# A transformer layer on one core: eight PSUM banks in one stock, and a first chunk transposed in two halves

## The chip, the core and the metric

The kernel runs on one core of a Trainium2 chip. The metric is the device time of one execution in microseconds (us). The engines are TensorE (PE; its weight loads are a row of their own, PEld), VectorE (DVE), ScalarE (ACT), GpSimd (POOL) and SyncE (SP), which issues most DMAs. PSUM, where matmuls write, has eight banks, each of 512 fp32 numbers on each of 128 partitions.

## The reference

```python
# x (1, 2048, 448); 16 heads of 28; F = 1792; every input is bf16
mod = silu(c) @ w_mod                      # six vectors of 448: sa, ca, ga, sb, cb, gb
h = layernorm(x) * (1 + ca) + sa
q, k, v = split(h @ wqkv)
# token s attends to s, s-2, s-4, ... s-14 (8 keys, those below 0 masked)
x = x + ga * (attention(q, k, v) @ wo)
h = layernorm(x) * (1 + cb) + sb
out = x + gb * (silu(h @ w1) @ w2)
```

## The kernel before

The 2048 tokens go through in four chunks of 512. Even and odd tokens are kept apart ("parity"), since the keys of a token have its own parity; a chunk is four tiles of 128 tokens, two of each parity. D = 448 is held as three k-tiles of 128 rows and a rest of 64, in an order of rows in which the two parities (or the two halves of F) use opposite halves of the rest tile, so that 64-row matmuls can run in pairs on the two halves of the array.

For each chunk: **norm1** (statistics per token, by DVE's `bn_stats` where `HOW1` has "b", by ACT's accumulating Identity and Square where it has "a"; a power on POOL for the reciprocal root; then the normalized tile xn), a transpose of xn (on PE for chunk 0, by DMA for the others), a modulation with (1 + ca) and sa that gives h; **project** (four groups ps_qk for q and k, cast to SBUF; two or three blocks ps_v). Attention goes in nine blocks b of up to 128 queries, for each parity: logits ps_l (16 small matmuls into two double tiles), Exp on ACT into p, a multiplication by a 0/1 mask on DVE, P.V on PE into ps_o with a column of ones for the sum, reciprocal and normalization on DVE into o, a DMA transpose into oT. Then **out_proj** (ps_wo, two tiles per 256 tokens, added to x by DVE), norm2, **ffn1** (seven groups ps_h of two 512-wide halves, Silu on ACT into hid) and **ffn2** (four tiles ps_y of 14 matmuls each, added to x by DVE into ot, stored by SP). The gates ga and gb are multiplied into wo and w2 beforehand, from two matmul groups ps_g.

A group with 64-row parts is made by `phases`: eight matmuls ("straight"), a drain that counts a semaphore, then six ("crossed") that wait for it. Other work can be queued between the two.

Everything is recorded as operations of a `Plan`, with their inputs and the buffers that they take and give back. What runs on each engine, and in which order, is written out in `ORDER`: a list of operation numbers, where a letter picks DVE (v) or ACT (a) for an operation that may run on either. Semaphores between engines are put in by the Tile framework from what each instruction reads and writes.

PSUM before: the pool `big` has three buffers of two banks (all groups of `phases`, the logits, the transposes of chunk 0, the warm-up matmuls), the pool `one` two buffers of one bank (P.V, ps_y, gates, modulation columns). The buffers turn round in the order in which they are asked for:

```python
    def bigt(name):
        return big.tile([128, 2, 512], F32, name=name, tag="big")

    def onet(name):
        return one.tile([128, 512], F32, name=name, tag="one")
```

Lines of the profile that matter here: L399 warm-up matmuls, L427 modulation columns, L443 gates, L524 transposes and L531/L533 their modulation, L561/L563 the padding of wqk into wp, L625 ps_qk, L645 ps_v, L673 ps_l, L681 Exp, L705 mask, L731 ps_o, L736/L737 reciprocal and normalization, L761 ps_wo, L764 its addition, L789 ps_h, L797 Silu, L809 ps_y, L814 its addition. ps_t is the tile of the transposes. When all is done a check of the sums picks, in case of extreme values, a slower path, which does not run here.

Of the kernel before, what the change touches and what calls it, by code (L numbers as in the profile page):

```python
# [7 lines left out]
BF16 = mybir.dt.bfloat16  # L8
F32 = mybir.dt.float32
# [27 lines left out]
WARM, JUNK = 7, 10  # L37
HOW1 = ("bbbb", "bbbb", "bbaa", "bbaa")
# [64 lines left out]
class Plan:  # L103
# [94 lines left out]

    def emit(self, order):
        self.rank()  # L200
        if order:
            seq = []
            for w in order.split():
                o = self.ops[int(w.rstrip("vap"))]
                o["eng"] = {"v": "dve", "a": "act", "p": "pool"}.get(w[-1], o["on"][0][0])
                seq.append(o)
            assert len(seq) == len(self.ops) == len({o["i"] for o in seq})
        else:
            _, got = self.order({o["i"]: o["rank"] for o in self.ops})
            seq = [self.ops[i] for i in got]  # L210
            for o in seq:
                o["at"], o["eng"], o["end"] = got[o["i"]]
        for o in seq:
            for r in o["take"]:
                o["slot"][r] = self.free[r].pop(0)
            o["fn"](o)
            for other, r in o["give"]:
                self.free[r].append(other["slot"][r])


def layer(ctx, tc, io, safe):
# [9 lines left out]
    big = ctx.enter_context(tc.tile_pool(name="big", bufs=3, space=PSUM))  # L231
    one = ctx.enter_context(tc.tile_pool(name="one", bufs=2, space=PSUM))
# [8 lines left out]
    def bigt(name):  # L241
        return big.tile([128, 2, 512], F32, name=name, tag="big")

    def onet(name):
        return one.tile([128, 512], F32, name=name, tag="one")
# [87 lines left out]
    P.resource("dma", 8)  # L333
    begin = P.op(("sp", 1630.0), none)
# [60 lines left out]
    def warm_up(n):  # L395
        if not warm:
            warm.append(bigt("ps_w"))
        for _ in range(n):
            T.matmul(warm[0][:, 0, :], lhsT=junk[:, 0:128], rhs=junk, start=True, stop=True)  # L399
    w_first = P.op(("pe", 600.0), none, take=("big",))  # L400
# [9 lines left out]
    def c_cols(o):  # L410
        box["c"] = one.tile([128, 512], F32, name="ps_c", tag="one")
        T.matmul(box["c"][:, 0:KT], lhsT=sc4[:], rhs=ident[0:KT, 0:KT], start=True, stop=True)
# [4 lines left out]
    def mod_cols(vecs, dst0, loads):  # L417
# [3 lines left out]
        def mm(o):  # L421
            ps[0] = one.tile([128, 2, KT], F32, name="ps_m", tag="one")
# [14 lines left out]
    def gate(i, v, loads):  # L437
        ps = {}

        def mm(o):  # L440
            ps[0] = onet("ps_g")
# [9 lines left out]
    class Norm:  # L451


        def __init__(self, us, src, after=(), n=2, how="bbbb", scratch=None):
# [14 lines left out]
            def mean(o, j):  # L469
# [11 lines left out]
            def shift(o, j, b):  # L481
# [13 lines left out]
            for j in range(0, 4, n):  # L495
                at, b = range(j, j + n), how[j] == "b"
                if b:
                    st = [P.op(("dve", 728.0), lambda o, j=i: stat(o, j), [src[us[i]]]) for i in at]
                    m = st
                else:  # L500
                    st = [P.op(("act", 600.0), lambda o, j=i: total(o, j), [src[us[i]]]) if how[j] == "a" else src[us[i]] for i in at]
                    m = [P.op(("dve", 62.0), lambda o, j=j: mean(o, j), st)]
                    st = [P.op(("act", 665.0), lambda o, j=i: square(o, j), m) for i in at]
                g = P.op(("dve", 62.0), lambda o, j=j: guard(o, j), st)
                r = P.op(("pool", 720.0), lambda o, j=j: rstd(o, j), [g])
                s = P.op(("dve", 62.0), lambda o, j=j, b=b: shift(o, j, b), [r])
                for i in at:
                    self.nr.append(P.op(either(704.0, 322.0), lambda o, j=i, b=b: norm(o, j, b), [r, s] + self.nr[:1], take=() if i else ("xn",)))

        def on_pe(self, order, out_of, view, waits, two=False):  # L510

            box, trs = self.box, []


            parts = ((0, 1), (2, 3)) if two else ((0, 1, 2, 3),)

            def tr(o, j):
                if j == 0:
                    for i in range(len(parts)):
                        box[i] = big.tile([128, KT // len(parts), 512], BF16, name="ps_t", tag="big")  # L520
                at = slice(128 * order[j], 128 * order[j] + 128)
                for i, ks in enumerate(parts):
                    for k in ks:
                        T.transpose(box[i][:, k - ks[0], at], box["x"][:, j, 128 * k:128 * k + 128], ident[:])  # L524

            def mod(o, i, ks):
                for k in ks:
                    out_, in_ = out_of(k), view(box[i][:, k - ks[0], :])
# [5 lines left out]
            for j in range(4):  # L534
                trs.append(P.op(("pe", 240.0), lambda o, j=j: tr(o, j), [self.nr[j]] + (trs[-1:] or self.after), take=() if j else ("big",) * len(parts),
                                give=((self.nr[0], "xn"),) if j == 3 else ()))
            self.done = []
# [407 lines left out]
```

## Time and profile before

| | us |
|---|---|
| median of three runs | 174.2 (173.69 to 174.68) |
| the profiled execution | 174.89 |
| its span | 173.2 |
| busy PE / ACT / DVE / POOL | 163.9 / 113.7 / 104.5 / 15.6 |
| first ps_v, first ps_qk, first ps_h start | 11.74, 14.40, 67.02 |
| last matmul ends | 168.7 |

The granted clock of PE is 0.999. Of the costliest groups, ps_y has 224 matmuls, ps_h 392, ps_qk 224, ps_wo 112, ps_v 126 and ps_o 288. The page gives busy time as a share of the span; matmuls are pipelined, so a matmul's own duration (0.35 us and more) is longer than the distance from one to the next, which is what counts in a dense stretch. In the slices, a digit is the busy share of a 4.33 us slice in tenths. In the timeline a row has start, duration, engine, line, operation, tiles, count, and in brackets the idle time before it with what ended it.

### The profile page before, as it was taken

The numbers are of one execution on the slowest core, as the hardware profiler recorded it, in microseconds if no ns is written. First come the engines' busy times: TensorE is split into PE (matmuls) and PEld (weight loads), VectorE is DVE, ScalarE is ACT, GpSimd is POOL, SyncE is SP. The second block draws the span as 40 slices with busy tenths as digits, with TensorE's granted clock in tenths as the row PEclk, the third lists the DMA queues.
The fourth block names the chain that finished last, engine by engine and source line by source line (L and its number), as shares of the span: only waits on it lengthen the run. The fifth ranks groups of instructions, "written<-read, shape, count | busy, mean of one in ns | idle before, by whom it ended". The sixth has DMA issues, their size and how long they took to land.

```text
span 173.2 us, 4260 instructions
## 1 busy us (share of the span) xinstructions
PE 163.9 (95%) x1770; PEld 81.0 (47%) x1771; DVE 104.5 (60%) x258; ACT 113.7 (66%) x157; POOL 15.6 (9%) x38
## 2 busy tenths in 40 slices
PE   7999999889999989999999999999999999999990
PEld 2544443345644544454554445555444444444540
DVE  5898988999999889328477325898361231100221
ACT  2269999977895845999998669644429933356000
POOL 3432311000001020002000000012001100000000
PEclk9999999999999999999999999999999999999999
DMA  5993999499935542001500303225200060200111
GB/s 181 341 308 89 225 234 257 149 240 141 318 81 127 143 97 53 4 0 25 126 2 4 81 0 83 54 57 113 61 28 28 1 149 30 80 0 2 32 57 36
DMA packets 33347, 17.47 MB, mean 101 GB/s; under 512 B 24297, under 2 KB 32937, under 8 KB 33321
## 3 DMA queue, kind: packets, MB, share of 16 engines
q1 hardware_dynamic: 33168, 16.90, 37.2%
q8 instruction: 16, 0.26, 0.7%
q10 hardware_dynamic: 152, 0.23, 0.5%
q14 instruction: 11, 0.08, 0.2%
HBM read 9.12 MB, written 1.84 MB: 63 GB/s over the span
## 4 chain that ended last, share of the span: by engine, by line
PE 70%; DVE 16%; DMA 7%; ACT 2%; POOL 2%; issue 2%; ACTq 0%
PE ps_y L809 25%; PE ps_h L789 25%; PE ps_wo L761 7%; DMA x_all<-in_A_x_dram 5%; PE ps_qk L625 4%; PE ps_v L645 3%; DVE st L463 3%; DVE p L705 2%; PE ps_o L731 2%; PE ps_l L673 2%; DMA oT<-o 2%; POOL rs L479 2%; DVE qk L629 2%; DVE o L737 1%; DVE x_all L764 1%
## 5 line engine op out<-in xcount | busy, mean ns | idle before, releaser
L809 PE MATMUL ps_y<-w,both 128*128 128x448 bf16 x224 | 44.7, 353 | 0.0
L789 PE MATMUL ps_h<-h,w 64*128 64x512 bf16 x392 | 44.3, 376 | 0.0
L797 ACT ACTIVATE both<-ps_h 128x1024 bf16<-128x1024 f32 x28 | 27.5, 1019 | 14.9 <-PE ps_h L789 14.6
L681 ACT ACTIVATE p<-ps_l 128x896 bf16<-128x896 f32 (+1 forms) x36 | 31.4, 927 | 5.8 <-PE ps_l L673 5.6
L809 PEld LDWEIGHTS <-both 128*128 128x128 bf16 x224 | 20.8, 98 | 20.2 <-issue 1.5
L789 PEld LDWEIGHTS <-w 64*128 64x128 bf16 x392 | 19.6, 94 | 21.8 <-issue 0.6
L814 DVE TENSOR_TENSOR ot<-ps_y,x_all 128x448 bf16<-128x448 f32 x16 | 10.0, 623 | 29.7 <-PE ps_y L809 29.6
L479 POOL TENSOR_TENSOR rs<-rs,negh 128x2 f32<-128x2 f32 x16 | 12.7, 793 | 120.0 <-DVE rs L476 82.4
L625 PE MATMUL ps_qk<-h,wp 64*128 64x512 bf16 x168 | 19.6, 377 | 0.5 <-ACT qk L629 0.4
L705 DVE TENSOR_TENSOR p<-p,maskb 128x1792 bf16<-128x1792 bf16 (+1 forms) x18 | 19.5, 1098 | 0.8 <-ACT p L681 0.8
L625 PEld LDWEIGHTS <-wp 64*128 64x128 bf16 x224 | 10.8, 94 | 13.4 <-issue 1.8
L473 ACT ACTIVATE screp<-x_all,mv 128x448 bf16<-128x448 bf16 x16 | 10.7, 666 | 4.3 <-DVE mv L470 4.1
L761 PE MATMUL ps_wo<-wo,oT 64*128 64x448 bf16 x112 | 12.7, 350 | 0.4 <-DMA oT<-o 0.4
L629 ACT CAST qk<-ps_qk 128x1024 bf16<-128x1024 f32 x10 | 9.9, 1007 | 3.7 <-PE ps_qk L625 3.7
L764 DVE SCALAR_TENSOR_TENSOR x_all<-ps_wo,x_all 128x448 bf16<-128x448 f32 x16 | 9.3, 620 | 4.5 <-PE ps_wo L761 4.5
L737 DVE TENSOR_TENSOR o<-ps_o,rc 112x448 bf16<-112x448 f32 (+1 forms) x18 | 11.2, 624 | 0.6
L645 PE MATMUL ps_v<-wv,h 64*128 64x448 bf16 x98 | 11.2, 350 | 0.4 <-ACT p L681 0.3
L731 PEld LDWEIGHTS <-p 128*128 128x128 bf16 x288 | 8.6, 96 | 5.3 <-DVE p L705 2.5
L731 PE MATMUL ps_o<-v,p 128*128 128x29 bf16 x288 | 10.0, 176 | 1.0 <-DVE p L705 0.9
L489 ACT ACTIVATE xn<-x_all,nm,rs 128x512 bf16<-128x512 bf16 x10 | 8.0, 807 | 3.6 <-DVE nm L482 3.2
L736 DVE RECIPROCAL rc<-ps_o 112x16 f32<-112x16 f32 (+1 forms) x18 | 4.5, 250 | 8.9 <-PE ps_o L731 8.9
L399 PE MATMUL ps_w<-both 128*128 128x512 bf16 x26 | 8.4, 479 | 1.3 <-DVE both L293 1.3
(85 smaller groups left out, 141.2 us busy)
## 6 DMA issues: line engine op xcount, KB each, us to landing
out_dram<-ot SPq DMA_DIRECT2D x16, 112.0 KB, 1.8
both<-in_w_mod_dram SPq DMA_DIRECT2D x2, 672.0 KB, 4.9
x_all<-in_A_x_dram SPq DMA_DIRECT2D x3, 448.0 KB, 5.7
w<-in_B_w_dram SPq DMA_DIRECT2D x3, 448.0 KB, 5.2
w<-in_B_w_dram SPq DMA_DIRECT2D x1, 896.0 KB, 7.1
both<-in_w_mod_dram SPq DMA_DIRECT2D x2, 336.0 KB, 5.5
w<-in_B_w_dram SPq DMA_DIRECT2D x1, 672.0 KB, 5.1
wv<-in_A_wqkv_dram SPq DMA_DIRECT2D x2, 224.0 KB, 5.6
```

The lines of the kernel that those rows point to most:

```text
L479: G.tensor_tensor(out=rs[:, j:j + n], in0=rs[:, j:j + n], in1=negh[:, 0:n], op=ALU.pow)
L625: return T.matmul(ps[:, j, :], lhsT=w.rearrange("p h d -> p (h d)"), rhs=h[rows, :, t, 128:128 + CP], start=start, stop=stop)
L629: copy_on(o)(out=qk[:, :, g, :, s0:s0 + CP], in_=ps[:].rearrange("p j (t s) -> p j t s", t=2))
L645: T.matmul(ps[:, par, 0:D], lhsT=h[rows, par, t, b0:b0 + 128], rhs=wv[rows, t, :], start=start, stop=stop)
L681: S.activation(out=out_, in_=ps[:, :, 0:4 * nq].rearrange("p j (g q) -> p j g q", q=nq), func=ACTF.Exp, scale=SCALE)
L705: V.tensor_tensor(out=p, in0=p, in1=maskb[:, 1 if b == 0 else 0, 0:nq].unsqueeze(1).to_broadcast([128, H, nq]), op=ALU.mult)
L731: T.matmul(ps[:, h, 0:DH + 1], lhsT=p[:, at:at + 128], rhs=v[:, h, 0:DH + 1], start=True, stop=True)
L737: V.tensor_tensor(out=box["o"][0:nq, off:off + D].rearrange("p (h d) -> p h d", d=DH), in0=ps[0:nq, :, 0:DH], in1=r.unsqueeze(2).to_broadc ...
L761: T.matmul(ps[:, par, 0:D], lhsT=oT[rows, t, par, s0:s0 + 128], rhs=wo[rows, par, t, :], start=start, stop=stop)
L789: return T.matmul(ps[:, j, :], lhsT=w, rhs=h[rows, :, t, :], start=start, stop=stop)
L797: silus[k].append(P.op(("act", 904.0), lambda o, i=i, box=box: S.activation(out=hid[:, k % 2, :, i, :], in_=box["ps"][:], func=ACTF.Silu), ...
L809: T.matmul(box["ps"][:, 0:D], lhsT=hid[:, k % 2, f % 2, f // 2, 128 * j:128 * j + 128], rhs=w2[:, f // 2 + 7 * (f % 2), :], start=(f == 0) ...
```

## The change

PSUM becomes four tiles of two banks, made once. A double tile is one of them, a single tile is half of one. Which of them an operation takes is written into `ORDER` behind a slash (0 to 3 for doubles, 0 to 7 for singles), so that the eight banks are one stock:

```diff
-    big = ctx.enter_context(tc.tile_pool(name="big", bufs=3, space=PSUM))
-    one = ctx.enter_context(tc.tile_pool(name="one", bufs=2, space=PSUM))
+    banks = ctx.enter_context(tc.tile_pool(name="banks", bufs=1, space=PSUM))
...
+    pairs = [banks.tile([128, 2, 512], F32, name=f"ps{i}") for i in range(4)]
+
+    def bigt():
+        return pairs[P.bank("big")]
+
+    def onet():
+        q = P.bank("one")
+        return pairs[q // 2][:, q % 2, :]
```

The output projection takes two singles instead of a double, and gives each back after its own addition. Chunk 0 is transposed and modulated in two halves of two tiles each, each in one bank, with eight modulations of 256 columns instead of four of 512; the V of block 0 needs the first half alone. The statistics of the fourth token tile move from DVE to ACT, and the warm-up shrinks:

```diff
-WARM, JUNK = 7, 10
-HOW1 = ("bbbb", "bbbb", "bbaa", "bbaa")
+WARM, JUNK = 7, 4
+HOW1 = ("bbba", "bbbb", "bbaa", "bbaa")
...
+        def on_pe(self, out_of, waits):
+            self.done = []
+            for i in range(2):
+                box, trs = {}, []
+                def tr(o, j, i=i, box=box):
+                    if j == 0:
+                        box["t"] = onet().bitcast(BF16).rearrange("p (k n) -> p k n", k=KT)
+                    for k in range(KT):
+                        T.transpose(box["t"][:, k, 128 * j:128 * j + 128], self.box["x"][:, 2 * i + j, 128 * k:128 * k + 128], ident[:])
...
-        box, first, m = phases(wo_mm, "ps_wo", D, need + wo_gated)
+        box, first, m = phases(wo_mm, D, need + wo_gated, True)
         for par in range(2):
-            x1_done[u + par] = P.op(("dve", 543.0), lambda o, par=par: add(o, par), [m])
-        P.op(("none", 0.0), none, [x1_done[u], x1_done[u + 1]], give=((first, "big"),))
+            x1_done[u + par] = P.op(("dve", 543.0), lambda o, par=par: add(o, par), [m] + ([x1_done[u]] if par else []), give=((first, "one"),))
...
-            box, first, m = phases(vmm, "ps_v", D, h1_done[k] + ([halo[k]] if k else []) + ld_v)
+            box, first, m = phases(vmm, D, (h1_part[0] if b == 0 else h1_done[k] + ([halo[k]] if k else [])) + ld_v)
```

`ORDER` is another list throughout, for all engines; the end of it, with ps_y tiles on singles 2, 3, 4 and 2 again (operations 754, 761, 747, 768) and their additions 758, 765, 751, 772:

```diff
+    "... 754/2 755 761/3 678 679 747/4 740 743 756 757 778 748 749 750 751 752 762 763 753 758 759 760 764 768/2 765 692 766 693 769 770 647 771 772 773 774 767 "
```

In it ACT normalizes one tile where it had ten, and casts six of the nine V blocks where it had four; DVE has the rest. On SP the load of the fourth chunk's x stands right behind that of the third.

More of the change, by code (lines that the diff above doesn't have):

```diff
@@ L197, in order, with bank @@
         return max(g[2] for g in got.values()), got
+    def bank(self, r):
+        return self.now[r].pop(0)
     def emit(self, order):
@@ L203, in emit @@
             for w in order.split():
+                w, *slots = w.split("/")
                 o = self.ops[int(w.rstrip("vap"))]
                 o["eng"] = {"v": "dve", "a": "act", "p": "pool"}.get(w[-1], o["on"][0][0])
+                o["banks"] = [int(x) for x in slots]
                 seq.append(o)
@@ L212, in emit @@
                 o["at"], o["eng"], o["end"] = got[o["i"]]
+        self.free["one"] = [6, 7]
         for o in seq:
+            o["held"] = {"big": [], "one": []}
             for r in o["take"]:
-                o["slot"][r] = self.free[r].pop(0)
+                if r not in o["held"]:
+                    o["slot"][r] = self.free[r].pop(0)
+                else:
+                    o["held"][r].append(o["banks"].pop(0) if order else self.free[r].pop(0))
+            self.now = {r: list(n) for r, n in o["held"].items()}
             o["fn"](o)
             for other, r in o["give"]:
-                self.free[r].append(other["slot"][r])
+                if r not in o["held"]:
+                    self.free[r].append(other["slot"][r])
+                elif not order:
+                    self.free[r].append(other["held"][r].pop(0))
 def layer(ctx, tc, io, safe):
@@ L333, in layer @@
     P.resource("dma", 8)
+    P.resource("pair", 4)
     begin = P.op(("sp", 1630.0), none)
@@ L395, in warm_up @@
     def warm_up(n):
-        if not warm:
-            warm.append(bigt("ps_w"))
         for _ in range(n):
             T.matmul(warm[0][:, 0, :], lhsT=junk[:, 0:128], rhs=junk, start=True, stop=True)
-    w_first = P.op(("pe", 600.0), none, take=("big",))
+    w_first = P.op(("pe", 600.0), lambda o: warm.append(bigt()), take=("big",))
     w_last = P.op(("pe", 213.0 * WARM), lambda o: warm_up(WARM), [w_first])
@@ L410, in c_cols @@
     def c_cols(o):
-        box["c"] = one.tile([128, 512], F32, name="ps_c", tag="one")
+        box["c"] = onet()
         T.matmul(box["c"][:, 0:KT], lhsT=sc4[:], rhs=ident[0:KT, 0:KT], start=True, stop=True)
@@ L421, in mm @@
         def mm(o):
-            ps[0] = one.tile([128, 2, KT], F32, name="ps_m", tag="one")
+            ps[0] = onet()[:, 0:2 * KT].rearrange("p (a k) -> p a k", a=2)
             for i, v in enumerate(vecs):
@@ L467, in total, with mean @@
                 S.activation(out=scratch, in_=x_all[:, us[j], :], func=ACTF.Identity, accum_out=sums[:, us[j]:us[j] + 1])
-            def mean(o, j):
+            def mean(o, j, n):
                 V.tensor_scalar(out=mv[:, j:j + n, 0], in0=sums[:, us[j]:us[j] + n], scalar1=-ROOT / D, scalar2=None, op0=ALU.mult)
@@ L495, in __init__ @@
             for j in range(0, 4, n):
[L496 to L499, printed above, removed]
-                else:
-                    st = [P.op(("act", 600.0), lambda o, j=i: total(o, j), [src[us[i]]]) if how[j] == "a" else src[us[i]] for i in at]
-                    m = [P.op(("dve", 62.0), lambda o, j=j: mean(o, j), st)]
-                    st = [P.op(("act", 665.0), lambda o, j=i: square(o, j), m) for i in at]
+                at, st, kinds = range(j, j + n), [], []
@@ new lines, in __init__ @@
+                same = len(set(how[j:j + n])) == 1
+                if same and how[j] != "b":
+                    st = [P.op(("act", 600.0), lambda o, j=i: total(o, j), [src[us[i]]]) if how[j] == "a" else src[us[i]] for i in at]
+                    m = [P.op(("dve", 62.0), lambda o, j=j: mean(o, j, n), st)]
+                    st = [P.op(("act", 665.0), lambda o, j=i: square(o, j), m) for i in at]
+                else:
+                    for i in at:
+                        if how[i] == "b":
+                            st.append(P.op(("dve", 728.0), lambda o, j=i: stat(o, j), [src[us[i]]]))
+                        else:
+                            m = P.op(("act", 600.0), lambda o, j=i: total(o, j), [src[us[i]]])
+                            m = P.op(("dve", 62.0), lambda o, j=i: mean(o, j, 1), [m])
+                            st.append(P.op(("act", 665.0), lambda o, j=i: square(o, j), [m]))
@@ L504, in __init__ @@
                 g = P.op(("dve", 62.0), lambda o, j=j: guard(o, j), st)
                 r = P.op(("pool", 720.0), lambda o, j=j: rstd(o, j), [g])
-                s = P.op(("dve", 62.0), lambda o, j=j, b=b: shift(o, j, b), [r])
+                if same:
+                    s = [P.op(("dve", 62.0), lambda o, j=j, b=how[j] == "b": shift(o, j, b, n), [r])] * n
+                else:
+                    s = [P.op(("dve", 62.0), lambda o, j=i, b=how[i] == "b": shift(o, j, b, 1), [r]) for i in at]
@@ L507, in __init__ @@
                 for i in at:
[L508 to L528, printed above, removed]
+                    self.nr.append(P.op(either(704.0, 322.0), lambda o, j=i, b=how[i] == "b": norm(o, j, b), [r, s[i - j]] + self.nr[:1], take=() if i else ("xn",)))
@@ L533, in mod @@
                         V.tensor_scalar(out=out_, in0=in_, scalar1=scale, scalar2=shift, op0=ALU.mult, op1=ALU.add)
[L534 to L537, printed above, removed]
-            for i, ks in enumerate(parts):
-                m = len(ks)
-                self.done.append(P.op(either(m * 670.0, m * 455.0), lambda o, i=i, ks=ks: mod(o, i, ks), trs + list(waits) + self.after, give=((trs[0], "big"),)))
-            self.trs = trs
+                for j in range(2):
+                    last = i == 1 and j == 1
+                    trs.append(P.op(("pe", 240.0), lambda o, j=j, tr=tr: tr(o, j), [self.nr[2 * i + j]] + trs[-1:] + (first if i and not j else []), take=() if j else ("one",),
+                                    give=((self.nr[0], "xn"),) if last else ()))
+                first = trs[-1:]
+                d = [P.op(either(455.0, 270.0), lambda o, k=k, mod=mod: mod(o, k), trs + list(waits)) for k in range(KT)]
+                P.op(("none", 0.0), none, d, give=((trs[0], "one"),))
+                self.done.append(d)
+            self.part, self.done = self.done[0], self.done[0] + self.done[1]
         def on_dma(self, dst, out_of, vec, waits):
@@ L591, in crossed @@
                     mm(box["ps"], part, kk, False, kk == 2, part)
-        a = P.op(("pe", 4 * step), straight, deps, take=("big",), mode=1)
+        a = P.op(("pe", 4 * step), straight, deps, take=("one", "one") if split else ("big",), mode=1)
         return box, a, P.op(("pe", 3 * step), crossed, [a], mode=1, lag=300.0)
     qk_done, v_of, v_take, v_op, qk_mm, v_mm, halo = {}, {}, {}, {}, {}, {}, {}
-    h1_done = {}
+    h1_done, h1_part = {}, {}
     def norm1(k):
@@ L631, in project @@
         for g in range(4):
-            box, first, m = phases(mm(g), "ps_qk", 512, h1_done[k] + pads)
+            box, first, m = phases(mm(g), 512, h1_done[k] + pads)
             qk_mm[k].append(m)
@@ L663, in mm @@
             for t in range(2):
-                held[t] = bigt("ps_l")
+                held[t] = bigt()
             for g in range(4):
@@ L722, in av @@
         def av(o):
-            ps = box["ps"] = one.tile([128, H, 32], F32, name="ps_o", tag="one")
+            ps = box["ps"] = onet().rearrange("p (h d) -> p h d", d=32)
             box["o"] = ob[par][o["slot"][f"o{par}"]]
@@ L760, in wo_mm @@
             rows = half(part if part is not None else par) if kk == 3 or part is not None else slice(0, 128)
[L761 removed]
+            T.matmul(ps[par][:, 0:D], lhsT=oT[rows, t, par, s0:s0 + 128], rhs=wo[rows, par, t, :], start=start, stop=stop)
         def add(o, par):
[L764 removed]
+            V.scalar_tensor_tensor(out=x_all[:, u + par, :], in0=box["ps"][par][:, 0:D], scalar=1.0, in1=x_all[:, u + par, :], op0=ALU.mult, op1=ALU.add,
                                    accum_out=sums[:, u + par:u + par + 1])
         need = [trs[b, par] for b in range(NB) for par in range(2) if q_of(b) < s0 + 128 and q_of(b) + nq_of(b) > s0]
[L767 removed]
+        box, first, m = phases(wo_mm, D, need + wo_gated, True)
         for par in range(2):
[L769 to L770 removed]
+            x1_done[u + par] = P.op(("dve", 543.0), lambda o, par=par: add(o, par), [m] + ([x1_done[u]] if par else []), give=((first, "one"),))
     f1_read, f2_read, silus = {}, {}, {}
@@ L793, in ffn1 @@
         for i in range(7):
-            box, first, m = phases(mm(i), "ps_h", 512, nrm.done + ld_1)
+            box, first, m = phases(mm(i), 512, nrm.done + ld_1)
             P.later(first, l_before)
@@ L806, in part @@
                 if f0 == 0:
-                    box["ps"] = onet("ps_y")
+                    box["ps"] = onet()
                 for f in range(f0, f1):
```

21 lines of the change are left out of this document (9 added, 12 removed), and 44 rows, old and new, of the table ORDER.

## The prediction

> **What bounds the kernel now.** I read the page first: engine totals, slices, chain. Then the timeline of PE alone, to find where it is not fed, and last the timeline of all engines at the places that the change touches.
>
> ```profile
> PE 163.9 (95%) x1770; PEld 81.0 (47%) x1771; DVE 104.5 (60%) x258; ACT 113.7 (66%) x157; POOL 15.6 (9%) x38
> ...
> PE   7999999889999989999999999999999999999990
> ...
> DVE  5898988999999889328477325898361231100221
> ACT  2269999977895845999998669644429933356000
> ...
> PE 70%; DVE 16%; DMA 7%; ACT 2%; POOL 2%; issue 2%; ACTq 0%
> ```
>
> A slice is 4.33 us. Up to slice 15 (65 us) DVE, ACT and PE are all near full: projections and attention. From there to the end only PE is: whatever holds PE there is added to the time. How dense PE is shows in the timeline of PE, tail first:
>
> ```profile
> 71.36 7.85 PE L789 MATMUL ps_h<-h,w 64*128 64x512 bf16 x70
> ...
> 147.23 10.75 PE L789 MATMUL ps_h<-h,w 64*128 64x512 bf16 x98
> 157.91 10.77 PE L809 MATMUL ps_y<-w,both 128*128 128x448 bf16 x56
> ```
>
> 98 matmuls from 147.23 to 157.91 are 0.109 us each, 56 of ps_y 0.191 each. At such rates (64-row ones with 448 columns 0.0955 by their columns, a set of logits 0.31, a P.V 0.5, gates 1.7, the second mod columns 0.9) the work from 71.5 to the last matmul at 168.7 is 96.3 us of 97.2: 0.9 is lost. From the first ps_qk (14.40) to 71.5 the work is 51.7 of 57.1: 5.4 is lost. So a better order can gain some 5 us up to 71 and almost nothing behind it.
>
> **Where the change binds.** The order and the waits of the built program show something that the diff does not say. Before, every PSUM tile comes out of its own buffer. Now all are halves or wholes of four tiles of two banks, and in the built program an instruction on one half of a pair waits for the last instruction of another engine on the other half. A ps_y group in bank 0.1 waits, between two of its own matmuls, for DVE's addition of the tile in 0.0; a P.V into half 1 waits for the normalization of the P.V in half 0; ACT's and DVE's readings of the two halves of transposes take turns. In before no such wait exists. Each turn is priced from the timeline of all engines:
>
> ```profile
> 102.69 0.82 PE L789 MATMUL ps_h<-h,w 64*128 64x512 bf16 x6
> 102.79 0.26 DVE L736 RECIPROCAL rc<-ps_o 112x16 f32<-112x16 f32 x1 [6.22 <-PE ps_o L731]
> 103.08 0.62 DVE L737 TENSOR_TENSOR o<-ps_o,rc 112x448 bf16<-112x448 f32 x1
> ...
> 107.30 0.38 PE L673 MATMUL ps_l<-qk 28*128 28x112 bf16 x16
> 107.41 0.62 DVE L814 TENSOR_TENSOR ot<-ps_y,x_all 128x448 bf16<-128x448 f32 x1 [0.23 <-PE ps_y L809]
> ```
>
> At 102.69 PE goes on behind a P.V; the normalization ends at 103.70. With 0.04 us from DVE to PE (a mask that ends at 63.63 lets PE go at 63.67) a P.V that must wait for it costs 1.05. Behind a ps_y (PE goes on at 107.30, the addition ends at 108.03) the same turn costs 0.77. What PE has queued between the two comes off.
>
> **Late stretch, PE alone (+8.2).** In the new order of PE: the second ps_y tile of chunk 0 goes on behind one set of logits: 0.77 - 0.31 = 0.46. Two P.V in a row and then ps_y in the partner half: the second P.V waits for an addition (0.27), and the ps_y behind both for two normalizations (1.25): 1.5. Two P.V in one pair: 1.05. ps_y behind a P.V in its pair: 1.05. Two ps_y tiles of chunk 1 sharing a pair: 0.77, and a P.V behind the second: 0.77. The last two P.V in one pair: 1.05. At the tail, where before ran 56 matmuls without a gap, two tiles share a pair: 0.77 twice, 1.54. Sum 8.19. Behind a waiting PE stand all later matmuls. Bounds: 6.5 if a third of the P.V turns is met by waits for masks or exps anyway, 10 if DVE has a mask (1.08, L705) ahead of two of those normalizations, as its order allows.
>
> **Start (+1.2).** Here are before's rows for it:
>
> ```profile
> 10.01 1.45 ACT L531 ACTIVATE h<-ps_t,modc 128x512 bf16<-128x512 bf16 x2 [0.38 <-PE ps_t L524]
> 11.12 0.99 DVE L533 TENSOR_SCALAR h<-ps_t,modc 128x512 bf16<-128x512 bf16 x2
> ...
> 11.74 2.82 PE L645 MATMUL ps_v<-wv,h 64*128 64x448 bf16 x28
> ...
> 13.64 0.92 ACT L561 COPY wp<-wqk 128x896 bf16<-128x896 bf16 x1
> ...
> 14.40 9.48 PE L625 MATMUL ps_qk<-h,wp 64*128 64x512 bf16 x84
> ```
>
> The fourth token tile's statistics move to ACT: 0.77 for the total, a second table load (1.28, mean of L351), 0.86 for the square. x lands at 4.14, so the total ends at 4.9 and the load at 6.2, when c has just come (before's Silu waited until 5.93): the load is hidden but for 0.2. The square stands ahead of the copy of scT, so mod columns start at 7.5 instead of 7.29. ACT normalizes one tile until 9.3, then modulates three quarters of the first half (0.38 each, between L414's 0.16 for 4 columns and L446's 0.54 for 448) to 10.4. The second half's transposes wait for these, though they write the other bank: 10.45 to 11.1. Then ACT, DVE, ACT in turns: the last quarter of the first half, free since 10, ends at 11.9; DVE does a tile's statistics (0.72) before the next two, to 13.25, ACT's last ends at 13.7. Two pads on ACT (0.92 each; before it had one) end at 15.5, and ps_qk starts at 15.6: +1.2. V of block 0 starts at 11.9, not earlier than 11.74. Without the turns it would be 10.5 and ps_qk 13.1: the bounds are -1.3 and, with slower short ACT instructions (0.67 as in L531), +2.8.
>
> SP's queue: the fourth x load moves up behind the third (before it waited until 17.28), and the gates' weights move behind the first two transposes of h, to some 19.5; at 5.5 to landing they are there at 25, before their gates at 29. POOL keeps its 16 pows of 0.79. Nothing of these ends last. Stores near the end go out late but land (1.8) before the last one; the tail behind the last matmul (4.5) stays.
>
> **Middle (+2.5).** I walk the new order with before's durations from 15.6. Forced turns: the second gate waits for DVE's copy of the first, behind an eviction and a modulation, 1.5; second mod columns 1.1; four P.V 0.7, 0.9, 0.95, 0.95. Sum 6.1. Other waits: 0.9 for the second chunk's modulated h, 0.4 at the first logits, 0.5 smaller ones: 1.8. Work 48.6, so FFN1 of chunk 0 starts at 15.6 + 48.6 + 7.9 = 72.1. The idle 7.9 stands against 5.4 before: +2.5. Bounds: -1 (the turns fall where ACT and DVE would be late anyway) to +6 (they come on top of before's 5.4). I take the walk. Moving nine normalizations (0.81) from ACT to DVE (0.41) is in it.
>
> Sum on the profiled execution: 174.89 (span 173.2 and 1.7 around it) + 1.2 + 2.5 + 8.2 = 186.8. That execution lies 0.7 above the median of 174.2, so I forecast **186.1**.
>
> **Rivals.** One: DVE and ACT set the middle as now, all of its turns are hidden behind them, and a third of the late P.V turns too. Their slices of 8 and 9 up to 65 us speak for it; against it, that PE lost 5.4 there for other reasons, and that behind 65 us hardly anything is late that could hide a turn. 174.2 + 1.2 - 1 + 6.5 = 180.9. Chance 0.18.
>
> Two, on the other side, that the change does what its words say: the turns cost nothing, because the other half's reader is always done when PE arrives. Then the start is -1.3, the middle idles 1.8 instead of 5.4 (-3.6), the late stretch keeps its 0.9: 174.2 - 4.9 = 169.3. It decides if a turn takes under 0.3 instead of 0.77 and 1.05. For it: the new order puts matmuls of other groups between the two parts of each group, better than before. Against it: ten places where the waiting instruction stands right behind what it waits for. Chance 0.08. [...]
>
> Three: the clock. The warm-up shrinks from 27 matmuls to 15, and PE has little between 9 and 11.9. Rows: the first 13 ps_w take 5.12 (0.39 each), the last 8 take 1.89 (0.24), so PE starts at about half speed and is full after 4 us of work. If it falls back, V of the first two blocks takes twice its 2.82, and as it ends with the pads, that is +2.8: 188.9. Chance 0.1. [...]
>
> **Numbers.** Forecast 186.1 with 0.6 (its own range, half way to the bounds, 182 to 190); one 0.18, three 0.1, two 0.08, and 0.04 for other faults. I give 178 to 190.5, leaving out two and the tops. This kernel's measurement tells about 0.5% from no change. Faster 0.08, same 0.02, slower 0.9.
>
> **What would show it.** Right: PE's waits after the change name DVE's o and ot, where now they hold only 0.9 for masks; ps_o behind o six or more times near 1.05 (two halves show as idle of PE or of its weight loads), ps_y behind ot some five times near 0.77, two of them in the last 5 us of matmuls; first ps_qk near 15.6, first ps_h near 72, PE under 90% busy. Wrong: PE without gaps behind 72 us, ps_qk before 14, or waits on DMA at the top of the chain.

## The result and the profile after

The changed kernel takes **192.61 us** (median of 4 runs, 191.33 to 194.81) against 173.96 for the kernel before (173.69 to 174.68): a ratio of 1.104, 95% interval 1.097 to 1.111. Forecast were 186.1 and slower; the sign was right, the time lies outside the range, 2.1 above its upper end. The profiled execution took 194.81 (span 193.1) and lies 2.2 above the median; it is read for where things happen, not for totals.

The page of the kernel after; PEclk is the granted clock of PE by slices of 4.83 us:

```profile
PE 167.9 (87%) x1759; PEld 81.5 (42%) x1759; DVE 106.1 (55%) x266; ACT 112.0 (58%) x158; POOL 15.5 (8%) x38
...
PE   7388997978979788999997996787999999999971
...
PEclk9979999995899996999999999999999999999999
...
PE 63%; DVE 18%; ACT 8%; issue 4%; DMA 3%; POOL 1%; SPq 1%; DVEq 0%; ACTq 0%
```

PE's share falls from 95 to 87%, with holes in every stage, and the clock dips in slices 2, 9, 10 and 15 (counted from 0). Who PE waits for (total us, times, longest):

```profile
PE ps L754 <- DVE o L760: 6.6, 6, 1.6
PE ps L831 <- DVE ot L836: 2.6, 4, 0.7
PE ps L831 <- DVE o L760: 2.2, 2, 1.1
PE ps L444 <- DMA both<-in_w_mod_dram: 1.8, 1, 1.8
PE ps L460 <- DVE gbc L463: 1.4, 1, 1.4
```

These are the turns that the prediction named: P.V (L754) and ps_y (L831) behind DVE's normalizations (o) and additions (ot). One of them, from the timeline of all engines, PE and DVE rows:

```profile
101.45 0.55 PE L754 MATMUL ps<-v,p 128*128 128x29 bf16 x16
...
102.33 0.55 PE L754 MATMUL ps<-v,p 128*128 128x29 bf16 x16 [0.33 <-DVE ot L836]
...
103.02 0.24 DVE L759 RECIPROCAL rc<-ps 112x16 f32<-112x16 f32 x1
103.29 0.62 DVE L760 TENSOR_TENSOR o<-ps,rc 112x448 bf16<-112x448 f32 x1
103.97 1.29 PE L831 MATMUL ps<-w,both 128*128 128x448 bf16 x6 [1.09 <-DVE o L760]
```

PE was done with the P.V at 102.88 and got ps_y's matmuls going at 103.97, 0.06 after the end of a normalization in the other half of the pair.

All traces can be cut at three places that every kernel here has: the first ps_qk, the 98th matmul of ps_h (end of FFN1 of chunk 0) and the last matmul. The kernels e1 to e11 are those of the experiments below; "half" counts the stretches of 3.41 us between 14 us and the last matmul in which the trace grants PE half its clock (middle + late).

| kernel | first ps_qk | from there to the 98th ps_h (middle) | to the last matmul (late) | half | span | median us |
|---|---|---|---|---|---|---|
| before | 14.40 | 65.86 | 88.07 | 0 | 173.2 | 173.96 |
| after | 17.73 | 74.22 | 96.75 | 3+0 | 193.1 | 192.61 |
| e1 by bank | 16.92 | 64.37 | 87.15 | 0 | 174.6 | 175.12 |
| e2 tail | 17.05 | 73.04 | 96.59 | 2+1 | 191.4 | 192.83 |
| e3 before, halves | 14.26 | 71.13 | 106.24 | 1+3 | 195.9 | 197.21 |
| e4 load order | 16.82 | 71.37 | 96.76 | 1+0 | 189.2 | 191.93 |
| e5 turns late only | 16.25 | 63.87 | 96.73 | 0 | 181.1 | 184.22 |
| e6 turns early only | 18.32 | 74.57 | 87.14 | 3+0 | 185.9 | 188.22 |
| e7 start by bank | 15.58 | 66.13 | 87.14 | 1+0 | 174.7 | 174.69 |
| e8 all | 13.74 | 64.23 | 87.15 | 0 | 170.6 | 172.73 |
| e9 hold where thin | 13.63 | 67.01 | 87.14 | 1+0 | 173.1 | 175.52 |
| e10 hold where dense | 13.58 | 64.81 | 89.13 | 0 | 173.0 | 174.80 |
| e11 warm-up alone | 16.61 | 76.16 | 96.75 | 4+0 | 194.0 | 194.62 |

Against before the change costs +3.3 at the start, +8.4 in the middle and +8.7 late: 20.4 in this execution, of which the tail behind the last matmul gives back 0.5. Forecast were 1.2, 2.5 and 8.2. (The forecast drew the line between middle and late at 71.5 of before and not at 80.26; between the two no loss was forecast.)

### The profile page after: what moved, and what is told of

Read it like the earlier page. It is cut to its first block, busy times and chain, and to the rows that moved or that the text cites. A ratio compares the mean times of both kernels' runs of the same rounds, so it can differ in the third digit from the quotient of the medians.

```text
span 193.1 us, 4277 instructions
## 1 busy us (share of the span) xinstructions
PE 167.9 (87%) x1759; PEld 81.5 (42%) x1759; DVE 106.1 (55%) x266; ACT 112.0 (58%) x158; POOL 15.5 (8%) x38
## 3 DMA queue, kind: packets, MB, share of 16 engines
HBM read 9.12 MB, written 1.84 MB: 57 GB/s over the span
## 4 chain that ended last, share of the span: by engine, by line
PE 63%; DVE 18%; ACT 8%; issue 4%; DMA 3%; POOL 1%; SPq 1%; DVEq 0%; ACTq 0%
PE ps L831 23%; PE ps L811 17%; PE ps L648 7%; PE ps L784 4%; PE ps L668 4%; DVE o L760 4%; DMA both<-in_w_mod_dram 3%; PE ps L754 3%; PE ps L696 3%; ACT screp L490 2%; DVE x_all L787 2%; DVE ot L836 2%; DVE xn L510 2%; DVE rc L759 2%; DVE w L863 1%
## 5 line engine op out<-in xcount | busy, mean ns | idle before, releaser
L831 PE MATMUL ps<-w,both 128*128 128x448 bf16 x224 | 45.2, 353 | 4.9 <-DVE ot L836 2.6
L811 PE MATMUL ps<-h,w 64*128 64x512 bf16 x392 | 43.3, 376 | 0.0
L704 ACT ACTIVATE p<-ps 128x896 bf16<-128x896 f32 (+1 forms) x36 | 31.6, 931 | 12.2 <-PE ps L696 10.7
L819 ACT ACTIVATE both<-ps 128x1024 bf16<-128x1024 f32 x28 | 27.2, 1021 | 18.0 <-PE ps L811 18.0
L831 PEld LDWEIGHTS <-both 128*128 128x128 bf16 x224 | 21.0, 98 | 25.4 <-issue 6.5
L648 PE MATMUL ps<-h,wp 64*128 64x512 bf16 x168 | 21.5, 400 | 0.4 <-ACT h L573 0.3
L754 PE MATMUL ps<-v,p 128*128 128x29 bf16 x288 | 10.1, 176 | 7.7 <-DVE o L760 6.6
L754 PEld LDWEIGHTS <-p 128*128 128x128 bf16 x288 | 8.7, 96 | 11.4 <-issue 10.9
L668 PE MATMUL ps<-wv,h 64*128 64x448 bf16 x98 | 12.0, 353 | 1.1 <-DVE h L554 0.7
L652 ACT CAST qk<-ps 128x1024 bf16<-128x1024 f32 x10 | 9.8, 1006 | 5.5 <-PE ps L648 5.5
L784 PE MATMUL ps<-wo,oT 64*128 64x448 bf16 x112 | 12.6, 350 | 0.2 <-DMA oT<-o 0.2
L760 DVE TENSOR_TENSOR o<-ps,rc 112x448 bf16<-112x448 f32 (+1 forms) x18 | 11.2, 624 | 0.6
```

The costliest lines, as they stand in the source:

```text
L648: return T.matmul(ps[:, j, :], lhsT=w.rearrange("p h d -> p (h d)"), rhs=h[rows, :, t, 128:128 + CP], start=start, stop=stop)
L668: T.matmul(ps[:, par, 0:D], lhsT=h[rows, par, t, b0:b0 + 128], rhs=wv[rows, t, :], start=start, stop=stop)
L704: S.activation(out=out_, in_=ps[:, :, 0:4 * nq].rearrange("p j (g q) -> p j g q", q=nq), func=ACTF.Exp, scale=SCALE)
L754: T.matmul(ps[:, h, 0:DH + 1], lhsT=p[:, at:at + 128], rhs=v[:, h, 0:DH + 1], start=True, stop=True)
L760: V.tensor_tensor(out=box["o"][0:nq, off:off + D].rearrange("p (h d) -> p h d", d=DH), in0=ps[0:nq, :, 0:DH], in1=r.unsqueeze(2).to_broadc ...
L784: T.matmul(ps[par][:, 0:D], lhsT=oT[rows, t, par, s0:s0 + 128], rhs=wo[rows, par, t, :], start=start, stop=stop)
```

## The experiments

**e1: the turns taken away.** Same order, same banks; a helper walks through the traced instructions and takes away each edge between two engines that comes only from the other bank of a pair, and adds one where the bank is the same (shortened here):

```diff
+    for x in nc.all_instructions():
+        ...
+        for i, b in banks_of(x):                      # pair, banks
+            for y, c, y_out, y_in in seen[i]:
+                if y.engine != x.engine and not set(b) & set(c) and not y_out & in_ and not out & y_in:
+                    tc.declare_no_dep(x, y, reason="other bank")
+            for n in b:
+                for e, y in last[i, n].items():       # last of each engine on this bank
+                    if e != x.engine:
+                        tc.add_manual_dep(x, y.name, SYNC, reason="same bank")
```

> The changed kernel, same order of every engine and same banks, but an instruction now waits only for those that touched its own bank: each edge between two engines that comes only from the other half of a pair is declared away, and edges of the same bank are kept. Theory (whole-pair tracking makes the turns, and the turns starve PE so that its clock falls in the middle): the late stretch loses its 8.2 us, the middle nearly all of the 8.4 that it lost against before, the start about 1 (the modulation columns were copied behind transposes of the other half); 192.6 becomes 175, in 173 to 178, and PE's waits no longer name o and ot. Rival A (the clock falls for another reason, the turns cost only themselves): 192.6 - 8.2 - 5.5 - 1 = 178, with a matmul stretch at half clock still there near 44 and 73 us. Rival B (the new order of the engines is what costs, the waits only show it): 186 or more.

Measured: 175.12 (174.16 to 178.36, 10 runs), ratio to before 1.001, interval 0.998 to 1.004. 17.5 of the 18.65 us that the change had cost are gone. Middle and late are now even shorter than before's (-1.5 and -0.9); the start is still 2.5 late, and the tail behind the last matmul is 1.3 longer, since the last additions wait 1.28 and 2.31 for stores to free their buffers. From its page:

```profile
PE 161.9 (93%) x1759; PEld 79.3 (45%) x1759; DVE 104.6 (60%) x266; ACT 111.6 (64%) x158; POOL 15.6 (9%) x38
...
PE   7299999989998999999999999999999999999960
...
PEclk9999999999999999999999999999999999999998
```

The holes and the dips of the clock went together, and no wait of PE names o or ot any more. Rival B, that the order is what costs, is out. The new order can lose the clock without its turns too, but less of it: e7 below, which has none either, loses one stretch.

**e3: the turns added to the old kernel.** The reverse: before's order and buffers, but its two single banks are halves of one tile (shortened).

```diff
-    one = ctx.enter_context(tc.tile_pool(name="one", bufs=2, space=PSUM))
+    both_one = one.tile([128, 2, 512], F32, name="ps_s")    # bufs=1
     def onet(name):
-        return one.tile([128, 512], F32, name=name, tag="one")
+        return both_one[:, P.cur["slot"]["one"], :]
```

> The kernel before, its order and all its buffers unchanged, except that the two single-bank buffers are the halves of one two-bank tile. Theory: the same turns appear in the old order: behind 65 us some 7 behind a P.V at 1.05 and 7 or 8 behind a ps_y at 0.77, +13 us (8 to 17), so 187. Rival (the order, not the sharing of a tile, makes the loss): 174 to 176.

Measured: 197.21, ratio 1.124 (1.116 to 1.131): 23 us for a change of one buffer. The mechanism is shown from the other side, and its size was again taken too small: 6.2 above the top of what was expected. Its waits for o, ot and one flag add up to 17.5 in all, and its four stretches at half clock would take 6.4 more at 1.6 each, which is an estimate: the forecast had no clock in it.

**e5 and e6: the turns in one part only.** e1's helper, applied only to instructions ahead of the first ps_h (e5) or only from there on (e6).

> The changed kernel with the waits by bank for every instruction ahead of the first ps_h, and by whole pair behind it. Theory: start and middle are those of e1 (first ps_qk near 17, 98th ps_h matmul near 81, no window at half clock between 14 and 82 us); the late stretch keeps its turns, 8 to 9.6 us, so 184 (182 to 186.5, the top with one window at half clock near 101). Rival A (the clock falls with the order, turns or not): windows at half clock near 43 and 73 remain, 187 or more. Rival B (the loss sits late): 190.

> The changed kernel with the waits by bank for every instruction from the first ps_h on, and by whole pair ahead of it. Theory: windows at half clock near 43 and 73 remain, the 98th ps_h matmul is near 90 as in the changed kernel, and from there to the last matmul it takes 87 us as in e1 instead of 96.8; 183 (181 to 185). Start and middle then cost about 8, the late stretch 9, and the two add up to the whole 17.5. Rival (the parts do not add: what is late early is caught up late): under 180.

Both have two runs only, so their totals are rough, and the stages say more. Measured: e5 184.22 (182.85 and 185.59), as the theory has it. e6 188.22 (187.58 and 188.86), above the 181 to 185: its middle and its late stretch are those expected (74.57 and 87.14), but its start was late (18.32) and its last store ended 1.4 later behind the last matmul than in after. The expectation had also started from the median of 192.6, while e6 shows the three stretches at half clock of the execution that took 194.81. By stages the two add up: turns and clock cost 9.6 late (96.73 against 87.15) and 9.9 to 10.2 in the middle, wherever the other part stands. The pages' clock, e5 first:

```profile
PEclk9969999999999999999999999999999999999998
```

```profile
PEclk9999999997599999699999999999999999999997
```

With the turns gone from the middle, the dips there are gone; with the turns kept there, they stay.

**e2: two of the turns at the tail.** Two of the last four ps_y tiles get banks of other pairs, and one of them (761) starts a few operations later.

```diff
-    ... 754/2 755 761/3 678 679 747/4 740 743 756 ... 768/2 765 ...
+    ... 754/2 755 678 679 747/4 740 743 761/0 756 ... 768/6 765 ...
```

> The changed kernel with other banks for two ps_y tiles of the last chunk (bank 0 of pair 0, and bank 0 of pair 3, behind their last Silu), so that no two of the last four share a pair; nothing else. Theory: two turns of 0.71 us go, -1.4 us, and the PE waits for ot in the last 8 us of matmuls are gone. Rival (PE would wait there for the stores' buffers or the additions anyway): no change.

Measured: 192.83, no change in the total. But the timeline of PE shows what the edit did:

```profile
176.26 10.77 PE L831 MATMUL ps<-w,both 128*128 128x448 bf16 x56
```

56 matmuls run without a gap, where after had these:

```profile
184.99 1.29 PE L831 MATMUL ps<-w,both 128*128 128x448 bf16 x6 [0.72 <-DVE ot L836]
...
187.00 2.05 PE L831 MATMUL ps<-w,both 128*128 128x448 bf16 x10 [0.71 <-DVE ot L836]
```

From the last ps_h to the last ps_y it takes 10.73 instead of 12.48, -1.75. In this execution another stretch at half clock, at 102.4, took 1.6 back ahead of it. A gain of 1.5 us can't be read from totals that vary by more (the four runs of e2 lie between 191.38 and 193.80, at mean granted clocks from 0.987 to 0.948); it can be read from the stage.

**e4, e7, e8: the start.** e4 issues the 672 KB load of w_mod ahead of the 112 KB one, as before did. e7 does so on top of e1, and gives the modulation of the first half to ACT alone, that of the second to DVE alone:

```diff
-    "75/0 76 78 0 5 8 11 1 7 ... 82 83/2 102 9 25 ...
-    "... 111a 114a 108v 113a 26 ... 117 121a 112v 159 118v 77 119v 68 167 120a 69 ...
+    "75/0 76 78 0 5 8 9 1 7 ... 82 83/2 102 11 25 ...
+    "... 111a 114a 108v 113a 112a 26 ... 117 121v 118v 119v 120v 159 77 68 167 69 ...
```

e8 adds warm-up matmuls and a fourth buffer for finished tokens:

```diff
-WARM, JUNK = 7, 4
+WARM, JUNK = 11, 4
+    outb.append(wp[:, 0, 0:14, :].rearrange("p h d -> p (h d)"))
         T.matmul(box["c"][:, 0:KT], lhsT=sc4[:], ...)
+        warm_up(4)
```

> The changed kernel with the two loads of the first part of w_mod issued in before's sequence (the 672 KB one ahead of the 112 KB one); nothing else. Theory for part of the start's loss: the modulation columns start near 7.3 instead of 8.55 us, the first ps_qk near 16.5 instead of 17.73, and the time falls by 1.2 us. Rival (the load is late because of the loads behind it, not of its place, or the middle swallows the gain): within 0.4 us of the changed kernel.

> e1 with the start mended: the 672 KB load of w_mod is issued first, and the modulation of the first tokens is parted by bank, ACT the first half and DVE the second, so that the two engines no longer take turns on one bank. Theory (the start lost to the load and to turns of ACT and DVE within a bank): first ps_qk near 14.5 instead of 16.9 and the time 172.8 (172 to 173.7). Rival A (the middle is bound by ACT and DVE and swallows it): 174.5 to 175.5. Rival B (the pads' weights land late, after 14 us): first ps_qk near 15.5, 174.

> e7 with 8 more warm-up matmuls (4 ahead of the copy of c, 4 behind it) and a fourth buffer for finished tokens, whose memory is that of the query weights, dead by then. Theory: the additions of the last two tiles no longer wait for stores (1.1 us), the clock is full from 9 us at the latest instead of 13 (0.4): 171.4 (170.5 to 172.5), a version faster than both. Rival: the last store's landing ends the kernel anyway and the warm-up changes nothing: as e7.

Measured: e4 191.93, 0.7 below after, which is less than the spread of either; its modulation columns start at 7.23, but the first ps_qk only at 16.82 instead of the 16.5 expected, between 0.2 and 0.9 earlier than in e2 and after, which have the same start. e7 174.69, ratio 0.999 (0.997 to 1.002): first ps_qk at 15.58 instead of the 14.5 expected. These are nearly the numbers of its rival B (15.5 and 174), but not for the reason given there: the pads waited only 0.27 for their weights and began at 11.34, and with the larger warm-up of e8 the first ps_qk comes 1.84 earlier. e8 **172.73**, ratio 0.992 (0.990 to 0.995): faster than both kernels, by 0.8% against before, and just above the 170.5 to 172.5 expected. The fourth buffer made the tail behind the last matmul 0.4 shorter than e7's, not 1.1. e8's start, from the timeline of PE:

```profile
8.40 0.61 PE L580 MATMUL ps<-ident,xn 128*128 128x128 bf16 x8
...
11.27 2.63 PE L702 MATMUL ps<-wv,h 64*128 64x448 bf16 x26 [0.23 <-ACT h L586]
13.74 0.38 PE L682 MATMUL ps<-h,wp 64*128 64x512 bf16 x2
```

Eight transposes take 0.61; in after they took 1.01 at half clock (row 9.42 below). The larger warm-up, which the change had cut, is worth 1.8 at the start here, not the 0.4 that I expected; 0.5 of this is lost again right behind, where PE waits for the pads.

**e11: the warm-up alone,** on the changed kernel with its turns.

> The changed kernel with 8 more warm-up matmuls (4 ahead of the copy of c, 4 behind it), everything else as changed, turns included. Theory (rival three of the prediction was part of it: the smaller warm-up leaves PE at half clock until 12 to 13 us): the clock is full from 6 to 9 us on, the first ps_qk comes at 16 to 16.5 instead of 17 to 17.7, the time falls by 1 to 1.5 us: 191.3. Rival A (the start is set by ACT and DVE alone): first ps_qk as before, no change. Rival B (the modulation columns' late load leaves a thin window anyway): the clock falls again near 9.

Measured: 194.62 (191.09 to 195.76), inconclusive as a total. The first ps_qk comes at 16.61, close to the 16 to 16.5 expected, but the profiled execution lost it in the middle, with four stretches at half clock instead of three. With the turns in place a better start can't be read from the total.

**e9 and e10: one wait by hand.** In e8, which has no half clock, PE is held once for two pows of GpSimd, at a place with small matmuls or among full ones.

```diff
+    def hold():
+        T.drain(fusable=True).then_inc(hold_a, 1)
+        G.wait_ge(hold_a, 1)
+        for _ in range(2):
+            G.tensor_tensor(out=idle[:], in0=epsb[:], in1=negh[:], op=ALU.pow)
+        G.drain(fusable=True).then_inc(hold_b, 1)
+        T.wait_ge(hold_b, 1)
```

> e8 with one wait put in by hand: ahead of the second P.V (near 36.4 us, among logits, P.V and one-column matmuls) PE waits until GpSimd, which it wakes, has done two pows, some 1.7 us. Theory (the clock is granted by windows of 3.41 us, and falls to half behind a window in which PE had less than some 0.35 of the matmul work that fits): the window there has 0.48 in e8 and gets 0.3 or less, so the next one is at half clock, and the span grows by the wait and 1.6 more: 170.6 + 3.3 = 173.9 by profile. Rival A (only a gap of a full window lets it fall): no half clock, + 1.7 or less: 172.3. Rival B (any gap of this length lets it fall): half clock here and in e10.

> e8 with the same wait in the middle of FFN1 of chunk 2 (near 124.5 us, among 98 full matmuls). Theory: the window keeps half of its work, the clock stays, and the last matmul comes later by the wait alone, 1.7 us: span 172.3. Rival B: half clock behind it, + 3.3, 173.9.

Measured: e9 175.52, ratio to before 1.008 (1.004 to 1.012); e10 174.80, ratio to before 1.001 (0.999 to 1.004). The 0.35 of the first was an estimate; what the stretches of the traces hold stands further below. Both are compared with e8 by their traces. Timeline of PE and stretches of granted clock (length, PE busy, matmuls, clock, DMA share, GB/s) of e9:

```profile
38.19 0.55 PE L803 MATMUL ps<-v,p 128*128 128x29 bf16 x16 [1.83 <-POOLq L376]
...
39.48 2.88 PE L697 MATMUL ps<-wqk,wp 64*128 64x512 bf16 x16
```

```profile
36.83:40.25 3.42, 2.06 (x56) 1.00 0.95 115
40.25:43.66 3.41, 3.41 (x34) 0.50 0.38 83
```

and of e10:

```profile
127.86 7.51 PE L860 MATMUL ps<-h,w 64*128 64x512 bf16 x68 [1.80 <-POOLq L376]
```

```profile
124.44:127.85 3.41, 1.62 (x16) 1.00 0.20 68
127.85:131.26 3.41, 3.40 (x32) 1.00 0.02 5
```

The same wait, 1.83 and 1.80: half clock behind it where the matmuls are small, none where they are full, although PE was busy for less there (1.62 against 2.06). In e9 sixteen ps_qk then take 2.88 instead of 1.90, so this stretch cost 1.0, not the 1.6 expected. Both spans came out at 173, where 173.9 and 172.3 were expected: e10's middle, which lies ahead of its wait, took 0.6 more than e8's. So the totals don't part the two, but the traces do: rival A fails in e9 and rival B in e10.

## Why the prediction was wrong

**Right: the turns.** That halves of a pair are tracked as one tile, which instructions it strikes, and its price. The late term was 8.2; the ten turns measure 0.48, 0.33, 1.09, 1.08, 1.07, 0.72, 0.72, 1.23, 0.72 and 0.71, together 8.15, and the stretch got 8.7 longer. e1, e3 and e5 show the cause. That 8.7 is so near is in part luck. Against e1, which has the same order without turns, the stretch is 9.6 longer, some 0.15 for each turn beyond the wait that the rows show (probably since in a dense stretch a row of 0.36 overlaps the next, which starts 0.19 later, and across a wait it does not). The new order gives back 0.9 of the 9.6, which the forecast had left as it was. Rival two, that they cost nothing, fell for the reason given against it. In e1, with waits by bank, no wait of PE names o or ot and the late stretch takes 87.15 instead of 96.75: the pair was a unit of the program alone.

**Failed: the middle, +2.5 forecast, +8.4 measured.** The term held three numbers. Turns 6.1: PE's waits of this kind add up to 6.7 in after. Five kernels have this middle with its turns, and it takes 71.37 with one stretch at half clock, 73.04 with two, 74.22 and 74.57 with three, 76.16 with four, 1.6 for each; 69.8 would be left with none, and e1 without turns takes 64.37, so the turns cost 5.4 by this estimate. Near enough; rival one, that they are hidden, falls with it (ACT's slices, which were read as near full up to 65 us, hold 5, 4 and 5 tenths in three of the last four). The new order without them was put at 1.8 of idle for before's 5.4. The 1.8 was right: in e1 PE is idle for 1.84 of this stage. But the 5.4 was a loss against the densest rates and no idle time; before's PE is idle for 3.16 there. So two different things were subtracted, and the order gains 1.5, not 3.6: 2.1 too hopeful. And a term that was missing: three stretches at half clock, 4.4. Together -1.5 + 5.4 + 4.4 = 8.3. The median execution lies 2.2 below this one, so it presumably has less of the last term.

The missing term is a fall of the clock in the middle; rival three had one at the start alone, where PE has little to do. It took no long gap: in after the longest one of PE near the first fall of the middle is 1.01:

```profile
39.80 0.38 PE L696 MATMUL ps<-qk 28*128 28x112 bf16 x16
40.11 0.56 PE L754 MATMUL ps<-v,p 128*128 128x29 bf16 x16
41.68 0.94 PE L444 MATMUL ps<-scT,both 128*128 128x1 bf16 x32 [1.01 <-DVE o L760]
42.48 0.55 PE L754 MATMUL ps<-v,p 128*128 128x29 bf16 x16
42.96 0.55 PE L696 MATMUL ps<-qk 28*128 28x112 bf16 x16
44.10 0.59 PE L754 MATMUL ps<-v,p 128*128 128x29 bf16 x16 [0.59 <-DVE o L760]
```

```profile
39.60:43.02 3.42, 2.41 (x88) 1.00 0.91 165
43.02:46.43 3.41, 2.82 (x43) 0.50 0.64 67
```

PE counts as busy for 2.41 of 3.42 us, but with matmuls that stream 112 columns on 28 rows, 29 columns, one column. At the full rate (ps_y: 448 columns on 128 rows in 0.191, so 0.426 ns a column) sixteen logits are 0.17 us of work and a P.V is 0.20; with a rest of V the stretch holds 0.22 of what fits. The turns thinned it out, and the next 6.8 us ran at half clock, full ps_qk among them.

Counted so (columns times rows over 128, each matmul's work spread evenly over its row) over all 13 traces, from 14 us to 12 us before the end, there are 561 stretches at full clock, 15 of them followed by half clock: the 12 with up to 0.36 of the work that fits all were, of the next ten, up to 0.40, three were, of the 539 above none. In after alone those with 0.22 and 0.32 were, those with 0.38 and 0.39 were not. Of the 20 stretches at half clock the five with up to 0.38 were followed by another, the 15 with 0.43 or more were not. These counts are not exact: at the edges of a stretch the work can be placed otherwise, which moves single values by some 0.05. By columns alone, without the rows, the two kinds don't part: one stretch with 0.78 lost the clock and one with 0.38 kept it. e9 (0.36) and e10 (0.47) fit, and so does the clearest case, in e7, where PE was never idle:

```profile
37.39:40.80 3.41, 3.41 (x118) 1.00 0.83 189
40.80:44.21 3.41, 3.41 (x32) 0.50 0.40 76
```

118 matmuls, nearly all of them small, hold 0.34. The same instructions stayed at full clock in e1 (0.57) and e8 (0.47), where the stretches happened to be cut otherwise. Where they lie differs from trace to trace: the first full one begins 5.62 us behind the start in before, 5.47 in after, 12.89 in e1 and 4.89 in e8, which are not whole steps of 3.41 apart. After's four runs took 194.81, 192.76, 192.46 and 191.33 us at mean granted clocks of 0.965, 0.973, 0.991 and 0.991; that the place of the stretches is one reason for such differences is my estimate, which no run parts from others.

**Failed: the start, +1.2 forecast, +3.3 measured.** Its rows in after:

```profile
8.55 1.00 PE L444 MATMUL ps<-scT,both 128*128 128x1 bf16 x32 [1.78 <-DMA both<-in_w_mod_dram]
9.42 1.01 PE L546 MATMUL ps<-ident,xn 128*128 128x128 bf16 x8
10.54 0.16 DVE L447 COPY modc<-ps 128x4 f32<-128x4 f32 x1 [1.94 <-PE ps L546]
...
10.86 1.47 ACT L552 ACTIVATE h<-ps,modc 128x256 bf16<-128x256 bf16 x3 [1.49 <-DVE modc L448]
```

The modulation columns began at 8.55, not 7.5: the walk let w_mod land as before, although its small part now goes out first. DVE's copy of them waited for transposes in the other half, a turn that I had overlooked. ACT took 0.49 for 256 columns where I had put 0.38. And the clock: at half from 8.88 to 12.30, behind a stretch (5.47 to 8.88) with less than 0.01 of the work that fits. So the thing that rival three feared did happen, at the transposes instead of V. Taking these away one after the other, the turns in e1, the order of the loads and the sharing of a half by ACT and DVE in e7, the small warm-up in e8, moved the first ps_qk from 17.73 (17.05 in e2) to 16.92, 15.58 and 13.74, which is 0.7 ahead of before.

**The range** was too narrow mainly for one reason: its bounds were sums of waits, with the rate of the work between them held fixed. Rival one at 180.9 and rival three at 188.9 were the only other prices, and three had the clock at one place only.

**Where the expected good of the change went.** It is there: in e8, without turns and with the start mended, the new order beats the old one by 0.8%. Not all of this is the order's own, since e8 has a fourth buffer too; e1's stages, 1.5 and 0.9 shorter than before's, are the order and its banks alone. Two things hid it: the pairs as tiles, and a slower start, made by the shortened warm-up, the order of two loads and the halves of the first chunk that ACT and DVE shared.

## What to carry to other kernels

Before two uses share a buffer, ask what the framework takes for one: here a stock of banks cut from two-bank tiles turned independent readers and writers into turns of 0.3 to 1.6 us. A wait on PE can cost more than its length where the work around it is small: here 1.83 us among small matmuls cost 1.0 more in the full ones behind it (e9), while behind 1.80 among full ones the clock stayed at 1.00 (e10). Busy time did not part the two, columns times rows in each 3.41 us did (0.36 and 0.47 of what fits). When single gains are smaller than the spread of the totals, cut the traces at fixed instructions and compare stage by stage.

## What the runs showed of the hardware that I had not expected

PE's clock was at half behind stretches of 3.41 us with little matmul work and no long gap: behind 0.22 of the work that fits in after (2.41 us busy, longest gap 1.01) and behind 0.34 in e7 ("busy" for all 3.41). Behind 0.47 in e10, with PE busy for 1.62, it stayed full. A stretch at half clock cost 1.0 (e9) to 1.8 us (e7 against e1, in the middle). The half clock stayed for up to three stretches in a row (10.2 us in e3), where the work in the stretch was again no more than 0.38. With eight more warm-up matmuls and no turns (e8) the clock was full from 4.9 us to the last matmul.
